# Two V stores of chunk 1 moved behind Wo's landing with one more buffer, and Wq's first quarter loaded in two halves of four heads

## The chip, the core and the metric

The kernel runs on one core of a Trainium2 chip. A core has five engines that run side by side: TensorE (PE, with its weight loads shown as PEld), VectorE (DVE), ScalarE (ACT), GpSimd (POOL) and SyncE (SP), which here does nothing but issue transfers. 16 DMA engines move data between the memory of the chip (DRAM), and the on-chip SBUF. Each engine takes its instructions in the order in which they were written for it and waits on semaphores of the others. The metric is the device time in microseconds (us), the median of several executions; lower is better.

## What is computed

The input x has 2048 rows of 512. A first block (A) normalizes the rows and runs a recurrent attention over 64 segments of 32 rows. A segment sees 8 memory rows and its own 32 rows; with 32 heads of 128 it forms queries, keys and values, a masked softmax and an output projection Wo. The first 8 rows of its output are the memory of the next segment, so the segments form a chain. A second block (B) is a gated MLP that mixes all rows by w_sp.

```python
for s in range(n_seg):
    h = concat([mem, xs], axis=1)            # 8 + 32 rows
    q, k, v = h @ Wq, h @ Wk, h @ Wv         # 32 heads x 128
    p = softmax(where(mask, q @ k.T * scale, -1e9))
    o = (p @ v) @ Wo
    mem = o[:, :M]                           # memory of the next segment
    outs.append(o[:, M:])
h = x + concat(outs)
h2 = h + B(layernorm(h))                     # gelu, spatial mix with w_sp, gate, w_out
```

All data is bfloat16 with float32 accumulation.

## The kernel before

**An emitter and its order.** The whole kernel is written as a list of operations (`Emitter.add`, line 53). Each names its engine and tokens for what it reads and writes; an operation waits for the last writer of each token that it reads, and for the last writer and all readers since of each token that it writes. A DMA is an operation of the engine that issues it (`sp`, line 274, for SP), is complete when it has landed, and counts as a reader of its source buffer until then. Within an engine the order is that of the calls.

**Loads at the start.** `load_xe` (line 301) brings the last 8 rows of each of the 16 segments of a chunk (a chunk is 16 segments). Wq, Wk, Wv and Wo are 4 MB each. `load_w` (line 305) loads a quarter, 8 of the 32 heads. The quarters of Wq (lines 318 to 321) are split by the rows of the contraction between the queues of SP and ACT; those of Wv and Wk (lines 896 to 899) go by SP alone, and the quarters of Wo (lines 921 to 923) by SP behind these. In DRAM the piece of one row of Wq, Wk or Wv that a quarter takes is 8 heads x 128 x 2 bytes; that of Wo is 512 x 2 bytes for each head and row.

**Work ahead of segment 0.** `start_group` (line 878) runs a group of matmuls into one of four PSUM banks and evacuates it on ACT or DVE in turn. `start_x` (line 889) calls `qkx_full` (line 443), which projects the rows of a chunk for four heads of Q (groups i = 0 to 7) or K (8 to 15); the matmuls are line 449. Its reads name the token of a quarter of the weight and, for Q, of its half on ACT's queue. `start_v` calls `vx_mm` (line 469, matmuls on line 476) and `vx_evac` (line 480).

**V of a chunk and its buffers.** `vx_evac(ck, n, ...)` copies group n of chunk ck to SBUF and stores it to DRAM (`vext_d`), from where `load_vx` (line 509) brings it back for each segment. Chunk 0 uses the eight slices of `part`; the other chunks take the two buffers of `Vs` in turn, by the counter `vcnt` (lines 484 to 486). A store of chunks 1 to 3 has 128 KB. For groups 2 to 7 of chunk 0 the rows of segments 2 to 5 are not stored at once: the calls are kept in `vrest[0]`, and line 1097 emits them in segment 0 with a wait for the landing of Wo's last quarter; `vrest[1]` holds the rest.

**Segment 0.** The loop over segments is at line 1015. In segment 0 the projections of the segment alternate with remaining groups of chunk 0. Line 1069 makes group 0 of chunk 1, (1,0), evacuated by DVE; line 1083 makes (1,1), evacuated by ACT at line 1096. Behind it SP gets the six stores of `vrest[0]`, `wT_read(0, 0)` (line 849, a transposing load of a block of w_sp) and `load_xe(3, 1)`; line 1106 adds the load of x block 2 (`load_x`, read by `ln_inplace`, statistics on line 367). Towards the end of the segment come (1,2), from the list `gx`, evacuated by DVE (line 490), and (2,0), from the list `gv`, evacuated by ACT (line 488) at line 1191. The output projection `Wo` (line 702) has its matmuls on line 708. Behind the evacuation of (2,0) ACT has, in this order, `S_mask(0)` (line 574), which fills the score bank of the next segment, and that segment's five `QK_evac` copies (line 550), which DVE transposes (line 558) for the score matmuls of `S_half` (lines 590 and 596). PE has the projections of the next segment (line 539) ahead of these scores.

**partx.** A buffer of 128 x 512 that `WoX_evac` (line 781) writes for the first time in segment 6 and `px_store` (line 772) stores.

Of the kernel before, what the change touches and what calls it, by code (L numbers as in the profile page):

```python
# [169 lines left out]
def fast_path(nc, st, keep, flags, A_x, A_mem0, A_Wq, A_Wk, A_Wv, A_Wo, A_seg_len, B_w_in, B_w_sp, B_b_sp, B_w_out, out):  # L170
# [3 lines left out]
    DH = A_Wq.shape[2]  # L174
# [21 lines left out]
    em = Emitter(n_dma_sems=40)  # L196

    def sb(name, shape, dt):
        return st.enter_context(nc.sbuf_tensor("f_" + name, shape, dt))
# [19 lines left out]
    hTe = sb("hTe", [128, NCK, DC, 128], BF)  # L219
# [12 lines left out]
    partx = sb("partx", [128, 512], BF)  # L232
# [38 lines left out]
    def PB(b):  # L271
        return ("ps", b)

    def sp(fn, **k):
        return em.add("sp", fn, dma=True, **k)

    def pe(fn, **k):
        return em.add("pe", fn, **k)

    def act(fn, **k):  # L280
        return em.add("act", fn, **k)

    def dve(fn, **k):
        return em.add("dve", fn, **k)
# [13 lines left out]
    def xbuf(j):  # L298
        return (xn[:, j, :], [("xn", j)]) if j < 2 else (part[:, j, :], [("part", j, 0), ("part", j, 1)])

    def load_xe(ck, j, queue="sp"):
        t, tok = xbuf(j)
        em.add(queue, lambda e: e.dma_start(t, xe[CK * ck:CK * ck + CK, XM:SEG, :]), dma=True, writes=tok)

    def load_w(mi, hq, queues=("sp",)):
        parts = len(queues)
        n = DC // parts
        wd, ws = ((A_Wq, w_q), (A_Wk, w_k), (A_Wv, w_v))[mi]
        wr = wd.rearrange("(dc p) h e -> p dc (h e)", p=128)
        cols = slice(hq * 8 * DH, (hq + 1) * 8 * DH)  # L310
        for k in range(parts):
            tok = ("W", mi, hq) if k == 0 else ("W", mi, hq, k)
            em.add(queues[k], lambda e, k=k: e.dma_start(ws[:, k * n:(k + 1) * n, cols], wr[:, k * n:(k + 1) * n, cols]), dma=True, writes=[tok])  # L313
            em.mark_const(tok)

    load_xe(0, 0)
    load_xe(1, 1, "act")
    for hq in range(4):
        load_w(0, hq, ("sp", "act"))
        if hq == 1:  # L320
            act(lambda e: e.preload_act_table_set("natural_log_exp_and_others"))
    load_x(0, 4)
# [120 lines left out]
    def qkx_full(ck, i, bank):  # L443
        mi, h0 = i // 8, 4 * (i % 8)
        ws = (w_q, w_k)[mi]
        for hh in range(4):
            h = h0 + hh
            for dc in range(DC):
                pe(lambda e, h=h, dc=dc, hh=hh: e.matmul(ps[:, bank, hh * 128:(hh + 1) * 128], lhsT=ws[:, dc, h * DH:(h + 1) * DH],
                                                         rhs=hTe[:, ck, dc, :], start=(dc == 0), stop=(dc == DC - 1)),  # L450
                   reads=[("hTe", ck), ("W", mi, h // 8) if mi or dc < 2 else ("W", mi, h // 8, 1)], writes=[PB(bank)])

    def qkx_full_evac(ck, i, bank, eng):
        mi, h0 = i // 8, 4 * (i % 8)
# [25 lines left out]
    def vx_evac(ck, n, bank, eng="act", queue="sp"):  # L480
        if ck == 0:
            t, tok = part[:, n, :], [("part", n, 0), ("part", n, 1)]
        else:
            j = vcnt[0] % 2
            vcnt[0] += 1
            t, tok = Vs[:, j, :], [("Vs", j)]
        if eng == "act":
            act(lambda e: e.activation(out=t, in_=ps[:, bank, :], func=ACT.Copy, scale=VSC), reads=[PB(bank)], writes=tok)
        else:
            dve(lambda e: e.tensor_scalar(out=t, in0=ps[:, bank, :], scalar1=VSC, scalar2=None, op0=ALU.mult), reads=[PB(bank)], writes=tok)  # L490
        def store(i0, i1, ks, queue="sp", after=()):
            r = slice(8 * i0, 8 * i1)
            dst = vext_d[ck, n, r, :, :].rearrange("p r e -> p (r e)")
            em.add(queue, lambda e: e.dma_start(dst, t[r, :]), dma=True, reads=tok, writes=[("vext", ck, n, k) for k in ks], after=after)

        if ck:
            store(0, CK, (0,), queue)
        else:
            store(0, 2, (0,), queue)
            if n < 2:  # L500
                store(2, CK, (1, 2))
            else:
                vrest[0].append(lambda after=(): store(2, 6, (1,), after=after))
                vrest[1].append(lambda: store(6, CK, (2,)))

    vcnt, vrest = [0], ([], [])
# [247 lines left out]
    def behind():  # L754
        return [em.by_eng["pe"][-1]]
# [19 lines left out]
    def px_load(rb):  # L775
        i0 = 4 * rb % 8
        for g in range(4):
            sp(lambda e, g=g: e.dma_start(part[32 * g:32 * g + M, i0:i0 + 4, :], px_d[rb, g].rearrange("j r d -> r j d")),
               reads=[("pxd", rb)] + [("part", i0 + j, k) for j in range(4) for k in range(2)], writes=[("pm", rb % 2, g)])
# [69 lines left out]
    def wT_read(i, k):  # L849
        r = slice(8 * k, 8 * k + 8)  # L850
        sp(lambda e: e.dma_start_transpose(out=wst[:, r, :], in_=B_w_sp[i * 64:(i + 1) * 64, 1024 * k:1024 * k + 1024]),
           writes=[("wst", k)], after=behind())
# [36 lines left out]
    def start_x(ck, i):  # L889
        start_group(qkx_full, qkx_full_evac, ck, i)  # L890

    def start_v(n, ck=0):
        start_group(vx_mm, vx_evac, ck, n)

    ln_apply(1)
    for hq in (0, 2, 1, 3):
        load_w(2, hq)
    for hq in range(4):
        load_w(1, hq)
# [21 lines left out]
    for hq in range(4):  # L921
        sp(lambda e, hq=hq: e.dma_start(w_o[:, 8 * hq:8 * hq + 8, :], wor[:, 8 * hq:8 * hq + 8, :]), writes=[("Wo", hq)])  # L922
        em.mark_const(("Wo", hq))


    class Gap:
# [23 lines left out]
    def vx_group(ck, n):  # L950
        gx.append([lambda dc=dc: vx_mm(ck, n, XB, dc) for dc in range(DC)] + [lambda: vx_evac(ck, n, XB, "dve")])

    def vx_atoms(ck, n):
        mms = [lambda ck=ck, n=n, dc=dc: vx_mm(ck, n, VXB, dc) for dc in range(DC)]
        gv.add(VXB, mms, lambda eng: vx_evac(ck, n, VXB, eng))
# [59 lines left out]
    for s in range(NSEG):  # L1015
# [3 lines left out]
            w2_load()  # L1019
        if j4 == 3 and rb > 0:  # L1020
            px_load(rb - 1)
        if s > 0:
            wT_read(s // 2, s % 2)

        def qk_piece(pi):
            QK(s, QKP[pi], range(2 if pi < 2 else 1 if pi == 2 and s else 0, DC))
# [67 lines left out]
        sm_rcp(1)  # L1094
        if s == 0:
            vx_evac(1, 1, 5, "act")
            for f in vrest[0]:
                f([em.last_w[("Wo", 3)]])
            wT_read(0, 0)
            load_xe(3, 1)  # L1100
        if s > 0:
            v_second()
        if j4 == 1:
# [210 lines left out]
    for i, rb in enumerate(order):  # L1314
# [8 lines left out]
        if i == 1:  # L1323
            pe(lambda e: e.matmul(ps[:, CB, :], lhsT=Sc[:], rhs=partx[:], start=True, stop=True),
               reads=["partx", "Sc"], writes=[PB(CB)])
# [52 lines left out]
    for tb in range(NTB):  # L1378
        for fb in range(len(ACC) if tb == 0 else 0, FB):
            bank = 5 + fb % 3 if tb == 0 else (tb * FB + fb) % 2  # L1380
# [688 lines left out]
def build_kernel(nc, A_x, A_mem0, A_Wq, A_Wk, A_Wv, A_Wo, A_seg_len, B_x, B_w_in, B_w_sp, B_b_sp, B_w_out, out):  # L2069
    args = (A_x, A_mem0, A_Wq, A_Wk, A_Wv, A_Wo, A_seg_len, B_w_in, B_w_sp, B_b_sp, B_w_out, out)  # L2070
    flags = {}
    with contextlib.ExitStack() as keep:
        with contextlib.ExitStack() as st:
            em, sems, dsems = fast_path(nc, st, keep, flags, *args)
# [83 lines left out]
```

## Time and profile before

| | us |
|---|---|
| median of 3 runs | 838.24 |
| lowest and highest | 837.37, 839.92 |
| the profiled execution | 840.62 |
| its span, first to last instruction | 838.9 |
| mean granted TensorE clock | 0.997 |

A row of the timeline has the start in us from the span's start, the time in us, the engine (with a q where only its sequencer works, as in issuing a DMA), the line of the kernel, the operation, what it writes and reads, the shape and how many in a row are merged; brackets show the idle time of the engine just before it and what ended it. A row of the chain of waits has start, time and what. A row of the windows has a stretch, the busy time and count of PE, PEld, DVE, ACT and POOL, then the granted clock, the busy share of the DMA engines and GB/s. A row of waits has the sum in us, how often, and the longest.

### The profile page before, as it was taken

To read this page: it belongs to the slowest core of one execution; us is meant where nothing else is said; L and a number is where in the kernel's file an instruction comes from. 1 tells how busy PE (TensorE), PEld (TensorE's weight loads), DVE (VectorE), ACT (ScalarE), POOL (GpSimd) and SP (SyncE) were. 2 spreads that over 40 slices of the span, in tenths; PEclk is the share of its full clock that TensorE was granted. 3 is DMA by queue.
4 is the path that set the end of the run, shared out by engine and by line. 5 is a ranking of instruction groups with operands and counts; after the bars stand their busy time and mean duration, and the time that the engine had idled before them with its cause. 6 is when DMAs were issued, how large, how long until landed. Compare 5 with 4: busy or idle time off the path is not lost.

```text
span 838.9 us, 48365 instructions
## 1 busy us (share of the span) xinstructions
PE 824.4 (98%) x21963; PEld 484.4 (58%) x21963; DVE 475.9 (57%) x1221; ACT 514.2 (61%) x1549; POOL 145.0 (17%) x412
## 2 busy tenths in 40 slices
PE   7999999999999999999999999999999999999998
PEld 7755565656566555655566656555665554444443
DVE  3546565656566555666556556565655576653344
ACT  2467777777777777777777777676666676300000
POOL 5202111121121111112211121111111123200000
PEclk9999999999999999999999999999999999999999
DMA  9975222122222222222212122333343278223101
GB/s 313 386 214 108 69 60 68 49 68 60 61 63 58 65 60 65 63 73 58 67 50 72 48 70 72 103 85 85 78 83 84 73 253 260 90 101 103 42 13 48
DMA packets 107652, 80.54 MB, mean 96 GB/s; under 512 B 49672, under 2 KB 97040, under 8 KB 107440
## 3 DMA queue, kind: packets, MB, share of 16 engines
q1 hardware_dynamic: 105712, 74.82, 30.8%
q8 instruction: 174, 2.85, 1.5%
q10 hardware_dynamic: 1504, 2.36, 0.9%
q14 instruction: 38, 0.31, 0.1%
q0 software_dynamic: 224, 0.20, 0.1%
HBM read 43.72 MB, written 23.13 MB: 80 GB/s over the span
## 4 chain that ended last, share of the span: by engine, by line
PE 92%; SPq 5%; DMA 1%; issue 0%; ACT 0%; DVE 0%; POOL 0%; POOLq 0%
PE f_ps L539 27%; PE f_ps L708 14%; PE f_ps L645 13%; PE f_ps L1266 12%; PE f_ps L426 4%; PE f_ps L764 4%; SPq L313 3%; PE f_ps L1360 3%; PE f_ps L1259 3%; PE f_ps L670 3%; PE f_ps L476 2%; PE f_ps L830 2%; PE f_ps L590 1%; DMA f_arena<-in_A_Wo_dram 1%; SPq L922 1%; PE f_ps L1226 1%
## 5 line engine op out<-in xcount | busy, mean ns | idle before, releaser
L539 PE MATMUL f_ps<-f_arena,f_hT 128*32 128x512 bf16 (+1 forms) x5120 | 238.5, 337 | 0.4
L539 PEld LDWEIGHTS f_ps<-f_arena,f_hT 128*32 128x32 bf16 x5120 | 124.4, 96 | 89.0 <-ACT f_hT L738 20.0
L550 ACT ACTIVATE f_Tst<-f_ps 128x512 bf16<-128x512 f32 (+2 forms) x320 | 143.4, 510 | 36.1 <-PE f_ps L539 28.5
L645 PE MATMUL f_ps<-f_arena,f_hT 128*32 128x512 bf16 x2048 | 139.8, 379 | 0.0
L708 PE MATMUL f_ps<-f_arena,f_cT 128*32 128x256 bf16 x4096 | 130.1, 273 | 2.2 <-DMA f_arena<-in_A_Wo_dram 1.3
L635 POOL TENSOR_TENSOR f_E_sb<-f_R_sb,f_E_sb 128x64 bf16<-128x64 f32 x128 | 47.5, 371 | 411.0 <-ACT f_R_sb L627 411.0
L708 PEld LDWEIGHTS f_ps<-f_arena,f_cT 128*32 128x32 bf16 x4096 | 97.0, 96 | 27.5 <-ACT f_cT L694 17.3
L558 DVE STREAM_TRANSPOSE f_QT<-f_Tst 128x256 uint32<-128x256 uint32 x128 | 57.1, 446 | 93.2 <-ACT f_Tst L550 93.2
L657 DVE TENSOR_SCALAR f_V_sb<-f_ps 128x512 bf16<-128x512 f32 (+1 forms) x128 | 71.4, 558 | 52.4 <-PE f_ps L645 52.4
L1266 PE MATMUL f_ps<-f_arena 128*128 128x512 bf16 x448 | 100.5, 379 | 0.0
L1266 PEld LDWEIGHTS f_ps<-f_arena 128*128 128x128 bf16 x448 | 43.7, 98 | 52.9 <-issue 0.3
L694 ACT ACTIVATE f_cT<-f_ps 128x160 bf16<-128x160 f32 (+1 forms) x192 | 55.6, 329 | 26.0 <-PE f_ps L676 25.4
L696 DVE TENSOR_SCALAR f_cT<-f_ps 128x256 bf16<-128x256 f32 x128 | 48.4, 420 | 36.7 <-PE f_ps L676 36.7
L604 ACT ACTIVATE f_E_sb<-f_ps 128x224 bf16<-128x224 f32 x128 | 46.3, 362 | 36.6 <-PE f_ps L616 35.4
L727 ACT ACTIVATE f_part<-f_ps 128x256 bf16<-128x256 f32 x128 | 49.3, 385 | 20.6 <-PE f_ps L708 16.1
L558 DVE STREAM_TRANSPOSE f_KT<-f_Tst 128x256 uint32<-128x256 uint32 (+2 forms) x192 | 58.4, 330 | 4.5 <-ACT f_Tst L550 1.8
L645 PEld LDWEIGHTS f_ps<-f_arena,f_hT 128*32 128x32 bf16 x2048 | 47.1, 95 | 19.8 <-issue 0.4
L738 ACT ACTIVATE f_hT<-f_ps 128x16 bf16<-128x16 f32 x126 | 23.3, 185 | 45.8 <-PE f_ps L735 45.8
L1272 DVE TENSOR_TENSOR f_arena<-f_ps,f_arena 128x512 f32<-128x512 f32 x28 | 19.3, 690 | 52.5 <-PE f_ps L1266 50.5
L627 ACT ACTIVATE f_R_sb<-f_R_sb 128x160 f32<-128x160 f32 x128 | 43.3, 338 | 4.0
L576 DVE CAST f_ps<-f_mask 128x224 f32<-128x224 bf16 x80 | 29.9, 373 | 26.9 <-ACT f_hT L406 24.5
L426 PE MATMUL f_ps<-f_arena,f_hTe 128*32 128x512 bf16 x640 | 41.9, 379 | 0.0
(127 smaller groups left out, 1157.8 us busy)
## 6 DMA issues: line engine op xcount, KB each, us to landing
wT_d<-f_wst SPq DMA_DIRECT2D x64, 128.0 KB
f_arena<-wT_d SPq DMA_DIRECT2D x32, 256.0 KB
f_arena<-in_A_Wv_dram SPq DMA_DIRECT2D x4, 1024.0 KB
f_arena<-in_A_Wk_dram SPq DMA_DIRECT2D x4, 1024.0 KB
f_arena<-in_A_Wo_dram SPq DMA_DIRECT2D x4, 1024.0 KB
f_Vx<-vext_d SPq DMA_DIRECT2D x62, 64.0 KB
vext_d<-f_Vs SPq DMA_DIRECT2D x24, 128.0 KB
zp_d<-f_Vs SPq DMA_DIRECT2D x20, 112.0 KB
```

The source lines that it names most:

```text
L426: pe(lambda e, c=c, rhs=rhs: e.matmul(ps[32 * c:32 * c + 32, bank, :], lhsT=hTe[:, ck, dc, 32 * sg:32 * sg + 32], rhs=rhs, start=(dc == 0) ...
L539: pe(lambda e, dc=dc, c=c, rhs=rhs: e.matmul(ps[32 * c:32 * c + 32, bank, 0:32 * nh], lhsT=hT[:, sl, dc, :], rhs=rhs, start=(dc == 0), sto ...
L550: act(lambda e: e.activation(out=st_.rearrange("p (hp i r) -> p hp i r", i=32, r=2), in_=ps[:, bank, 0:64 * np_].rearrange("p (hp r i) -> ...
L558: dve(lambda e: e.transpose(out=dst, in_=src), reads=tok, writes=[(nm, b, k) for k in halves(b, p0, np_)])
L635: pool(lambda e: e.tensor_tensor(out=ev, in0=rv, in1=ev, op=ALU.mult), reads=[("R", b), ("Ex", b)], writes=[("Ex", b)])
L645: pe(lambda e, dc=dc, c=c, c0=c0: e.matmul(ps[32 * c:32 * c + 32, bank, 0:w], lhsT=hT[:, sl, dc, :], rhs=w_v[:, dc, c0:c0 + w], start=(dc ...
L657: dve(lambda e: e.tensor_scalar(out=dst, in0=src, scalar1=VSC, scalar2=None, op0=ALU.mult), reads=[PB(bank)], writes=tok)
L694: act(lambda e: e.activation(out=dst, in_=src, func=ACT.Copy, scale=UNSC), reads=[PB(bank)], writes=tok)
L696: dve(lambda e: e.tensor_scalar(out=dst, in0=src, scalar1=UNSC, scalar2=None, op0=ALU.mult), reads=[PB(bank)], writes=tok)
L708: pe(lambda e, h=h, g=g, i=i, b=b, c=c: e.matmul(ps[32 * g:32 * g + 32, bank, 0:d1 - d0], lhsT=cTh[:, i, 8:40], rhs=w_o[:, h, d0:d1], star ...
L727: act(lambda e: e.activation(out=part[:, s % 8, d0:d1], in_=ps[:, bank, 0:d1 - d0], func=ACT.Copy), reads=[PB(bank)], writes=[("part", s % ...
L1266: pe(lambda e: e.matmul(ps[:, bank, 0:TB], lhsT=z2[:, sc, fb * 128:(fb + 1) * 128], rhs=wTb[tb % 2][:, :, sc, :], start=first, stop=last), ...
```

## The change

`load_w` can load half of a quarter's heads (`u` is 0 or 1), and Wq's first quarter is loaded so: four DMAs, each of half the bytes, in place of two. Group i = 0 of Q reads the token of the first half alone.

Group (1,0) is put in `partx` in place of a buffer of `Vs`, so that the counter of `Vs` starts with (1,1). The six stores of `vrest[0]` are emitted right behind the loads of Wo, ahead of the loop over segments, still with their wait for Wo's last quarter; SP takes its DMAs in order, so the stores of (1,0) and (1,1) now follow them. `wT_read(0, 0)` and `load_xe(3, 1)` are emitted at the top of segment 0 and stay behind the six stores.

```diff
--- before.py
+++ after.py
@@ -302,21 +302,22 @@
         t, tok = xbuf(j)
         em.add(queue, lambda e: e.dma_start(t, xe[CK * ck:CK * ck + CK, XM:SEG, :]), dma=True, writes=tok)
 
-    def load_w(mi, hq, queues=("sp",)):
+    def load_w(mi, hq, queues=("sp",), u=None):
         parts = len(queues)
         n = DC // parts
         wd, ws = ((A_Wq, w_q), (A_Wk, w_k), (A_Wv, w_v))[mi]
         wr = wd.rearrange("(dc p) h e -> p dc (h e)", p=128)
-        cols = slice(hq * 8 * DH, (hq + 1) * 8 * DH)
+        cols = slice(hq * 8 * DH, (hq + 1) * 8 * DH) if u is None else slice(4 * u * DH, 4 * (u + 1) * DH)
         for k in range(parts):
-            tok = ("W", mi, hq) if k == 0 else ("W", mi, hq, k)
+            tok = ("Wh", k) if u == 0 else ("W", mi, hq) if k == 0 else ("W", mi, hq, k)
             em.add(queues[k], lambda e, k=k: e.dma_start(ws[:, k * n:(k + 1) * n, cols], wr[:, k * n:(k + 1) * n, cols]), dma=True, writes=[tok])
             em.mark_const(tok)
 
     load_xe(0, 0)
     load_xe(1, 1, "act")
     for hq in range(4):
-        load_w(0, hq, ("sp", "act"))
+        for u in (None,) if hq else (0, 1):
+            load_w(0, hq, ("sp", "act"), u)
         if hq == 1:
             act(lambda e: e.preload_act_table_set("natural_log_exp_and_others"))
     load_x(0, 4)
@@ -448,7 +449,7 @@
             for dc in range(DC):
                 pe(lambda e, h=h, dc=dc, hh=hh: e.matmul(ps[:, bank, hh * 128:(hh + 1) * 128], lhsT=ws[:, dc, h * DH:(h + 1) * DH],
                                                          rhs=hTe[:, ck, dc, :], start=(dc == 0), stop=(dc == DC - 1)),
-                   reads=[("hTe", ck), ("W", mi, h // 8) if mi or dc < 2 else ("W", mi, h // 8, 1)], writes=[PB(bank)])
+                   reads=[("hTe", ck), ("Wh", dc // 2) if i == 0 else ("W", mi, h // 8) if mi or dc < 2 else ("W", mi, h // 8, 1)], writes=[PB(bank)])
 
     def qkx_full_evac(ck, i, bank, eng):
         mi, h0 = i // 8, 4 * (i % 8)
@@ -480,6 +481,8 @@
     def vx_evac(ck, n, bank, eng="act", queue="sp"):
         if ck == 0:
             t, tok = part[:, n, :], [("part", n, 0), ("part", n, 1)]
+        elif (ck, n) == (1, 0):
+            t, tok = partx[:], ["partx"]
         else:
             j = vcnt[0] % 2
             vcnt[0] += 1
@@ -921,6 +924,8 @@
     for hq in range(4):
         sp(lambda e, hq=hq: e.dma_start(w_o[:, 8 * hq:8 * hq + 8, :], wor[:, 8 * hq:8 * hq + 8, :]), writes=[("Wo", hq)])
         em.mark_const(("Wo", hq))
+    for f in vrest[0]:
+        f([em.last_w[("Wo", 3)]])
 
 
     class Gap:
@@ -1019,8 +1024,9 @@
             w2_load()
         if j4 == 3 and rb > 0:
             px_load(rb - 1)
-        if s > 0:
-            wT_read(s // 2, s % 2)
+        wT_read(s // 2, s % 2)
+        if s == 0:
+            load_xe(3, 1)
 
         def qk_piece(pi):
             QK(s, QKP[pi], range(2 if pi < 2 else 1 if pi == 2 and s else 0, DC))
@@ -1094,10 +1100,6 @@
         sm_rcp(1)
         if s == 0:
             vx_evac(1, 1, 5, "act")
-            for f in vrest[0]:
-                f([em.last_w[("Wo", 3)]])
-            wT_read(0, 0)
-            load_xe(3, 1)
         if s > 0:
             v_second()
         if j4 == 1:
```

## The prediction

> **What bounds the kernel now.** I read the page first, then the chain of waits, then the rows of each engine in the first 70 us, where every edit lies.
>
> ```profile
> span 838.9 us, 48365 instructions
> PE 824.4 (98%) x21963; PEld 484.4 (58%) x21963; DVE 475.9 (57%) x1221; ACT 514.2 (61%) x1549; POOL 145.0 (17%) x412
> ```
>
> PE is busy for 98% of the span, so a gain is either idle PE time removed or nothing. The chain of waits has PE to itself from 55.01 us on; before that it runs back through SP's loads:
>
> ```profile
> 42.84 12.13 DMA f_arena<-in_A_Wo_dram
> 55.01 1.38 PE f_ps L708 x44
> ...
> 57.40 3.05 PE f_ps L539 x72
> ```
>
> Wo's last quarter, whose issue starts at 42.84, lands at 42.84 + 12.13 = 54.97, and that landing starts everything behind it. The timeline shows the PE waits that the change touches (the second row is of the weight loads):
>
> ```profile
> 10.65 1.57 PE L449 MATMUL f_ps<-f_hTe,f_arena 128*128 128x128 bf16 x16 [3.31 <-DMA f_arena<-in_A_Wq_dram]
> 31.21 3.17 PEld L476 LDWEIGHTS f_ps<-f_arena,f_hTe 128*32 128x32 bf16 x64 [0.33 <-issue]
> 53.17 0.55 PE L708 MATMUL f_ps<-f_arena,f_cT 128*32 128x256 bf16 x12
> 55.01 1.38 PE L708 MATMUL f_ps<-f_arena,f_cT 128*32 128x256 bf16 x44 [1.29 <-DMA f_arena<-in_A_Wo_dram]
> 57.25 3.20 PE L539 MATMUL f_ps<-f_arena,f_hT 128*32 128x512 bf16 x72
> 60.28 0.27 PE L590 MATMUL f_ps<-f_QT,f_KT 128*32 128x40 bf16 x16
> ```
>
> PE waits 3.31 us for Wq's first quarter and 1.29 us for Wo's last. The 60.28 row is the first score matmul of segment 1.
>
> **Wq's first quarter in halves.** Each half asks for half the bytes, so group 0 can start earlier than 10.65, by 3.31 us at the very most (the whole wait) and by 0 at least. Either end is worth 0 on the end of the kernel: PE only reaches the 55.01 wait sooner, and Wo's landing ends that. What covers the lead is this wait of 1.29 us, which grows by it; without that cover the lead would count. The start is chased by loads throughout:
>
> ```profile
> 15.00:41.00 26.00, 26.00 (x468) 20.73 (x466) 14.96 (x34) 12.68 (x27) 8.61 (x25) 1.00 1.06 383
> 41.00:51.00 10.00, 10.00 (x239) 7.15 (x240) 4.43 (x11) 5.80 (x15) 1.23 (x3) 1.00 1.08 332
> 51.00:55.00 4.00, 2.44 (x80) 1.03 (x71) 1.22 (x5) 1.99 (x8) 1.18 (x4) 1.00 0.52 174
> ```
>
> The last two columns are the DMA engines' busy share and GB/s: they are full until 51 us. The halves do not change the bytes, but a row piece of Wq shrinks from 8 heads (2 KB) to 4 (1 KB). Wv and Wk move in 2 KB pieces (first row, 383 / 1.06 = 361 GB/s per full share), Wo in 1 KB pieces (second row, 332 / 1.08 = 307). By these 1.05 MB would take 3.42 instead of 2.90 us, +0.5 us on all behind it; the second stretch also holds other transfers, so I take **+0.2 us** on Wo's landing.
>
> The two added DMA issues (one on SP, one on ACT) cost 3.35 / 4 = 0.8 and 2.19 / 2 = 1.1 us of queue time:
>
> ```profile
> 1.56 3.35 SPq L313 DMA_DIRECT2D f_arena<-in_A_Wq_dram  x4
> 2.71 2.19 ACTq L313 DMA_DIRECT2D f_arena<-in_A_Wq_dram  x2
> 6.83 0.60 ACT L411 ACTIVATE f_hTe<-f_ps 128x512 bf16<-128x512 bf16 x1 [2.87 <-PE f_ps L387]
> 19.78 0.68 DVE L367 BATCH_NORM_STATS2 f_st<-f_part 128x6 f32<-128x512 bf16 x1
> ```
>
> ACT idles 2.87 us before its first work, which hides its issue and the table load behind it; the x loads pushed on SP are first read at 19.78. If that cover were gone, it would be up to 1.1 us of a start that Wo's landing hides anyway. Nothing for both.
>
> **The V stores behind Wo.** Today SP issues two 128 KB stores of chunk 1's V, (1,0) and (1,1), before it blocks on Wo's landing; the six held-back stores of chunk 0 follow, then a transposing load of w_sp, the x rows of chunk 3, x block 2:
>
> ```profile
> 50.15 2.17 SPq L494 DMA_DIRECT2D vext_d<-f_Vs  x2
> 54.99 3.31 SPq L494 DMA_DIRECT2D vext_d<-f_part  x6
> 58.34 1.33 SPq L851 DMA_TRANSPOSE f_wst<-in_B_w_sp_dram  x1
> 59.71 0.57 SPq L303 DMA_DIRECT2D f_xn<-in_A_x_dram  x1
> 60.33 0.58 SPq L295 DMA_DIRECT2D f_xn<-in_A_x_dram  x1
> 61.72 1.80 SPq L494 DMA_DIRECT2D vext_d<-f_Vs  x2
> 63.57 0.92 SPq L494 DMA_DIRECT2D vext_d<-f_part  x2
> ```
>
> After the change the blocking six stand ahead of everything in segment 0, so (1,0) and (1,1) come last: at 60.33, where x block 2 stands now, and 0.92 / 2 = 0.46 us later, at **60.8**. That is 9 us later than now for (1,1).
>
> Does Wo land earlier without them? At most by their bytes: 0.262 MB / 332 GB/s = 0.8 us. But (1,0) was queued after Wo and landed after it:
>
> ```profile
> 55.36 0.69 DVE L490 TENSOR_SCALAR f_Vs<-f_ps 128x512 bf16<-128x512 f32 x1 [1.59 <-DMA vext_d<-f_Vs]
> 57.57 0.59 ACT L488 ACTIVATE f_Vs<-f_ps 128x512 bf16<-128x512 f32 x1
> 58.05 0.37 ACT L574 ACTIVATE f_ps<-f_mask 128x224 f32<-128x224 bf16 x1
> 58.55 2.32 ACT L550 ACTIVATE f_Tst<-f_ps 128x512 bf16<-128x512 f32 x5
> 59.18 0.45 DVE L558 STREAM_TRANSPOSE f_QT<-f_Tst 128x256 uint32<-128x256 uint32 x1 [3.13 <-ACT f_Tst L550]
> ```
>
> DVE's wait for that store ended at 55.36, behind 54.97. So I take 0 of the 0.8. The Trainium skill, "DMA: Bandwidth & Descriptors", section "Queues, rings and completion order", speaks against this part of the change: on each DMA engine one queue's descriptors are consumed in ring order, so a store queued behind Wo would take nothing from it; by that rule the sum keeps the 0, by bytes alone it would be 0.8 us less.
>
> **The buffer that the hold keeps.** The Vs pair now rotates one step earlier: (1,1) takes Vs 0, (1,2) takes Vs 1, and the next, (2,0), takes Vs 0 again. Today (1,2) takes Vs 0 (DVE's 1.59 us wait above) and (2,0) takes Vs 1, free by then: the 57.57 row shows no wait. DVE's wait goes and is worth 0, as DVE idles 3.13 us before its next work at 59.18. In its place ACT's copy of (2,0) must wait until (1,1)'s store, issued at 60.8, has landed. How long a 128 KB store takes is bounded by SP's own wait on the stores of partx:
>
> ```profile
> SPq L778 <- DMA px_d<-f_partx: 23.1, 12, 2.8
> 115.79 0.32 SPq L773 DMA_DIRECT2D px_d<-f_partx  x1
> 118.88 1.31 SPq L778 DMA_DIRECT2D f_part<-px_d  x4
> ```
>
> The mean is 23.1 / 12 + 0.32 = 2.2 us, the slowest 2.8 + 0.3 = 3.1; in a full queue (1,0) took 55.36 − 50.15 = 5.2. The queue after 55 is nearly empty but holds the transposing load and x rows, so I take 2.5: landing at **63.3** (63.0 to 66.0).
>
> ACT works in order. Behind the copy stand the mask of score bank 3 (L574) and the five copies of Q and K (L550); behind these DVE's transposes and PE's scores, and PE, in order too, has only the 72 projection matmuls (57.25 + 3.20 = 60.45) before them. From ACT's copy to the scores it takes 60.28 − 57.57 = 2.71 us now; I take 2.65, as the projections will be done. Scores at 63.3 + 2.65 = 65.95 against 60.28: **+5.7 us**, of PE idle with nothing to hide it (5.4 to 8.4 by the bounds). Zero is excluded unless the store lands before 57.57.
>
> **The clock after such a gap.** These rows are busy time by engine with PEclk third from the end:
>
> ```profile
> 7.60:11.00 3.40, 0.35 (x7) 0.38 (x8) 0.00 (x0) 0.00 (x0) 2.38 (x13) 1.00 1.04 375
> 11.00:14.40 3.40, 3.40 (x36) 3.40 (x34) 0.89 (x2) 0.60 (x2) 2.37 (x11) 0.50 1.05 399
> 14.40:17.80 3.40, 3.40 (x63) 3.40 (x62) 1.49 (x4) 1.84 (x4) 2.65 (x11) 1.00 1.06 360
> 52.00:55.40 3.40, 2.10 (x80) 1.28 (x84) 0.93 (x4) 1.08 (x5) 0.64 (x2) 1.00 0.35 123
> ```
>
> After 3.4 us in which PE worked 0.35, the granted clock stood at 0.50 for 3.4 us, and PE did 36 matmuls instead of 63: 3.4 x (1 − 36/63) = 1.5 us lost. A stretch with 2.10 us of work lost nothing. A gap from 60.45 to 65.95 holds such an empty stretch, but part of the slow time may still lie in the gap: 0 to 1.5, I take **+1.2 us**. The Trainium skill, "TensorE: Matmul & The Clock Gate", Part 1, has windows of 3413 ns that run freely and halve the rate after an idle one; by it the loss depends on the window's phase, between 0.7 and 1.7 us, and the sum would stay within 0.5 us.
>
> Other moved steps: w_sp's transposing load and the x rows of chunk 3 keep their place behind the six stores, worth 0; x block 2 is issued about 0.95 us later, and DVE reads it in segment 1, itself 5.7 us later, worth 0 (uncovered 0.95). Partx is written next in segment 6; its store then is the 115.79 row.
>
> **Sum.** 5.7 + 1.2 + 0.2 + 0 = +7.1 us. The profiled execution took 840.62 us, its span 838.9; the median is 838.24, and I add the difference to that: **845.3 us**.
>
> **The rivals.**
> 1. *The stall without the clock loss.* For it: the slow stretch may fall inside the gap or not come. Against: the 0.50 row. 838.24 + 5.9 = 844.1.
> 2. *A longer stall.* The store lands in a full queue as (1,0) did: 66.0, scores at 68.65, +8.4; with 0.2 and 1.5 that is 848.3. For it: load of w_sp ahead of it. Against: only 174 GB/s even before 55.
> 3. *Not slower: Wo lands early.* The place is Wo's last quarter: from 51 to 55 the share is 0.52, so some DMA engines finish late, and if the two stores hold these up, Wo may come far sooner. PE then gains its 1.29 us: 836.95. As SP's line takes 63.3 − 54.97 = 8.3 us from Wo's landing to the store's, this decides only if Wo lands by 57.57 − 8.3 = 49.3, 5.7 us earlier; 0.8 us is what the bytes are worth.
> 4. *The change does not do what it says:* the hold keeps no buffer in the way, because ACT's copy is ordered otherwise, and Wo lands as before: 838.4. Against: the 1.59 us that DVE waits for just such a store now.
>
> **How the numbers follow.** Forecast 0.60, rival 1 0.20, rival 2 0.10, rival 3 0.04, rival 4 0.06. The range of 842.0 to 848.3 takes in the first three with their bounds (Wo 0.8 us earlier, a store 0.5 us quicker). A measurement can tell about 0.3%, 2.5 us, from no change. Slower holds the first three, 0.90; rivals 3 and 4 lie within 0.3%, except that the halves' lead might add to rival 3: same 0.07, faster 0.03.
>
> **What would show it.** ACT's L488 at about 63 with an idle of some 5.5 us put down to DMA vext_d<-f_Vs; SP's row for f_Vs x2 at about 60.3, behind the f_part x6; PE idle before L590 of segment 1; PEclk 0.50 for a stretch after 64; PE's first L449 before 10.65 and a longer wait for Wo. Wrong would be an ACT copy at 57.6 without a wait, or Wo landing before 54.

## The result and the profile after

| | before | after |
|---|---|---|
| median of 6 runs each, us | 837.75 | 846.29 |
| lowest and highest, us | 837.31, 839.92 | 844.42, 848.59 |
| the profiled execution, us | 840.62 | 844.42 |
| its span, us | 838.9 | 842.7 |

The changed kernel is slower: ratio 1.010, 95% interval 1.0082 to 1.0119. The profiled execution of after, 844.42, is the lowest of its six, and that of before, 840.62, lies above all six of its times, so the two spans differ by 3.8 us where the medians differ by 8.5. The time is therefore read stage by stage.

The chain of waits of after, from 30 to 76 us, still has Wo's landing in it; a V store (`DMA vext_d<-f_Vs`) now stands there too, as the shares by line show:

```profile
by line: DMA f_arena<-in_A_Wo_dram 26.5%; SPq L925 19.6%; PE f_ps L542 11.8%; PE f_ps L477 10.1%; PE f_ps L648 7.5%; PE f_ps L711 7.5%; DMA vext_d<-f_Vs 4.4%; ACT f_Tst L553 2.2%; SPq L497 1.8%; ACT f_part L491 1.3%; ACT f_Vs L491 1.3%; SPq
```

PE's timeline of after (line numbers have moved by 1 to 3: L450 is the Q and K projection of a chunk, L711 is Wo, L542 the projections of a segment, L593 the scores):

```profile
8.29 1.86 PE L450 MATMUL f_ps<-f_hTe,f_arena 128*128 128x128 bf16 x16 [0.73 <-DMA f_arena<-in_A_Wq_dram]
29.72 3.64 PE L477 MATMUL f_ps<-f_arena,f_hTe 128*32 128x512 bf16 x64 [0.46 <-issue]
53.90 1.39 PE L711 MATMUL f_ps<-f_arena,f_cT 128*32 128x256 bf16 x44 [1.39 <-DMA f_arena<-in_A_Wo_dram]
56.14 3.20 PE L542 MATMUL f_ps<-f_arena,f_hT 128*32 128x512 bf16 x72
64.21 0.32 PE L593 MATMUL f_ps<-f_QT,f_KT 128*32 128x40 bf16 x16 [4.87 <-DVE f_KT L561]
73.66 3.20 PE L542 MATMUL f_ps<-f_arena,f_hT 128*32 128x512 bf16 x72
```

The first group starts at 8.29 in place of 10.65, and PE still waits 1.39 us for Wo. New is the gap of 4.87 us ahead of segment 1's scores. DVE's transpose ended it, but the reason stands one engine further back, in ACT's timeline:

```profile
56.38 0.18 ACT L741 ACTIVATE f_hT<-f_ps 128x16 bf16<-128x16 f32 x1 [0.37 <-PE f_ps L738]
61.83 0.60 ACT L491 ACTIVATE f_Vs<-f_ps 128x512 bf16<-128x512 f32 x1 [5.27 <-DMA vext_d<-f_Vs]
62.32 0.36 ACT L577 ACTIVATE f_ps<-f_mask 128x224 f32<-128x224 bf16 x1
62.60 2.31 ACT L553 ACTIVATE f_Tst<-f_ps 128x512 bf16<-128x512 f32 x5
```

ACT stands 5.27 us before the copy of (2,0), until the store of (1,1) out of the same Vs buffer has landed. SP's timeline shows why that store is late:

```profile
53.88 3.24 SPq L497 DMA_DIRECT2D vext_d<-f_part  x6
57.16 1.32 SPq L854 DMA_TRANSPOSE f_wst<-in_B_w_sp_dram  x1
58.53 0.57 SPq L303 DMA_DIRECT2D f_xn<-in_A_x_dram  x1
59.15 0.58 SPq L497 DMA_DIRECT2D vext_d<-f_partx  x1
59.78 0.43 SPq L497 DMA_DIRECT2D vext_d<-f_Vs  x1
60.25 0.46 SPq L295 DMA_DIRECT2D f_xn<-in_A_x_dram  x1
```

The six stores start when Wo has landed, and (1,1) is issued at 59.78, 5.9 us behind that. It lands at 61.83, after 2.05 us. The windows of after (last three columns: granted clock, DMA share, GB/s; the first number after the length is PE's busy time) show the second cost:

```profile
4.90:8.30 3.40, 1.43 (x20) 1.06 (x18) 1.79 (x6) 0.60 (x1) 2.51 (x8) 1.00 0.95 296
8.30:11.70 3.40, 3.40 (x33) 3.40 (x34) 0.89 (x2) 0.60 (x1) 2.35 (x12) 0.50 1.05 400
59.50:62.90 3.40, 0.00 (x0) 0.00 (x0) 0.00 (x0) 1.07 (x3) 0.00 (x0) 1.00 0.70 231
62.90:66.30 3.40, 2.09 (x56) 1.02 (x60) 1.96 (x6) 2.17 (x6) 0.00 (x0) 0.50 0.44 125
66.30:69.70 3.40, 3.40 (x72) 1.52 (x60) 1.70 (x4) 1.91 (x6) 0.92 (x3) 0.50 0.09 27
69.70:73.10 3.40, 3.40 (x136) 2.21 (x128) 2.27 (x6) 1.64 (x7) 0.45 (x2) 1.00 0.26 79
```

A stretch without any PE work is followed by two at half the clock: 72 matmuls where the next stretch does 136. From segment 1's scores to the 72 projections of segment 2 it takes 73.66 − 64.21 = 9.45 us. In the profile of before that end point is this row of PE's timeline, 7.14 us behind the scores at 60.28:

```profile
67.42 3.20 PE L539 MATMUL f_ps<-f_arena,f_hT 128*32 128x512 bf16 x72
```

So the half clock cost 2.31 us in this profile. By segment 2 the changed kernel is 73.66 − 67.42 = 6.24 us behind. What follows is the same code in both, 838.9 − 67.42 = 771.5 us before and 842.7 − 73.66 = 769.0 after: the rest of the program took 2.5 us less in the profile of after, and no edit lies there.

### The profile page after: what moved, and what is told of

It reads as the page before. It is cut to its first block, busy times and chain, and to the rows that moved or that the text cites. A ratio compares the mean times of both kernels' runs of the same rounds, so it can differ in the third digit from the quotient of the medians.

```text
span 842.7 us, 48369 instructions
## 1 busy us (share of the span) xinstructions
PE 826.1 (98%) x21963; PEld 487.2 (58%) x21963; DVE 475.2 (56%) x1221; ACT 512.8 (61%) x1549; POOL 144.5 (17%) x412
## 3 DMA queue, kind: packets, MB, share of 16 engines
q10 hardware_dynamic: 1776, 2.36, 0.9%
## 4 chain that ended last, share of the span: by engine, by line
PE 94%; DMA 3%; SPq 1%; ACT 1%; issue 0%; DVE 0%; ACTq 0%
PE f_ps L542 26%; PE f_ps L711 14%; PE f_ps L648 13%; PE f_ps L1268 11%; PE f_ps L427 4%; PE f_ps L767 4%; PE f_ps L477 3%; PE f_ps L1362 3%; PE f_ps L1261 3%; PE f_ps L673 3%; PE f_ps L450 2%; PE f_ps L833 2%; PE f_ps L593 1%; DMA f_arena<-in_A_Wo_dram 1%; PE f_ps L1228 1%; SPq L925 1%
## 5 line engine op out<-in xcount | busy, mean ns | idle before, releaser
L542 PE MATMUL f_ps<-f_arena,f_hT 128*32 128x512 bf16 (+1 forms) x5120 | 238.3, 337 | 0.2
L542 PEld LDWEIGHTS f_ps<-f_arena,f_hT 128*32 128x32 bf16 x5120 | 126.9, 96 | 86.9 <-ACT f_hT L741 19.5
L648 PE MATMUL f_ps<-f_arena,f_hT 128*32 128x512 bf16 x2048 | 141.6, 383 | 0.2 <-issue 0.2
L711 PE MATMUL f_ps<-f_arena,f_cT 128*32 128x256 bf16 x4096 | 130.0, 273 | 1.8 <-DMA f_arena<-in_A_Wo_dram 1.4
L711 PEld LDWEIGHTS f_ps<-f_arena,f_cT 128*32 128x32 bf16 x4096 | 96.4, 96 | 27.3 <-ACT f_cT L697 18.3
L648 PEld LDWEIGHTS f_ps<-f_arena,f_hT 128*32 128x32 bf16 x2048 | 47.9, 96 | 20.6 <-issue 1.3
L593 PEld LDWEIGHTS f_ps<-f_QT,f_KT 128*32 128x32 bf16 x2048 | 28.3, 95 | 23.5 <-DVE f_KT L561 22.9
```

The costliest lines, as they stand in the source:

```text
L542: pe(lambda e, dc=dc, c=c, rhs=rhs: e.matmul(ps[32 * c:32 * c + 32, bank, 0:32 * nh], lhsT=hT[:, sl, dc, :], rhs=rhs, start=(dc == 0), sto ...
L648: pe(lambda e, dc=dc, c=c, c0=c0: e.matmul(ps[32 * c:32 * c + 32, bank, 0:w], lhsT=hT[:, sl, dc, :], rhs=w_v[:, dc, c0:c0 + w], start=(dc ...
L711: pe(lambda e, h=h, g=g, i=i, b=b, c=c: e.matmul(ps[32 * g:32 * g + 32, bank, 0:d1 - d0], lhsT=cTh[:, i, 8:40], rhs=w_o[:, h, d0:d1], star ...
```

## The experiments

Two theories: *theory 1*, ACT's copy of (2,0) waits for the held store of (1,1), PE idles behind it and its clock falls; *theory 2*, the loss is in the smaller pieces of Wq's halves or in SP's order as such. Edits are against the changed kernel unless said otherwise, ratios against the kernel before on the same chip.

| run | ratio, 95% interval | median, us | before, us |
|---|---|---|---|
| the kernel before again | 0.9995, 0.9979 to 1.0010 | 839.76 | 839.46 |
| the halves alone | 1.0004, 0.9989 to 1.0019 | 840.53 | 839.46 |
| the hold undone | 0.9993, 0.9977 to 1.0008 | 838.80 | 839.46 |
| own buffer for (1,1) | 1.0023, 1.0008 to 1.0038 | 841.69 | 839.46 |
| own buffers for (1,1), (1,2) | 1.0028, 1.0006 to 1.0050 | 838.59 | 836.71 |
| two loads later | 1.0050, 1.0033 to 1.0067 | 839.98 | 836.71 |
| the hold alone | 1.0106, 1.0083 to 1.0128 | 843.79 | 836.71 |
| gap filled, 18 matmuls | 1.0123, 1.0106 to 1.0140 | 845.43 | 836.71 |
| the changed kernel again | 1.0064, 1.0039 to 1.0089 | 847.24 | 842.43 |
| gap filled, 12 matmuls | 1.0054, 1.0035 to 1.0072 | 846.65 | 842.43 |

**The kernel before again.**

> The kernel before, unchanged, to see how far two executions differ and where Wo's last quarter lands in another one. Both theories: ratio 1.000 within 0.003, PE's wait for Wo between 0.5 and 2 us, Wo landing within 1.5 us of 54.97, no PE idle over 1 us after it.

PE's timeline has one row for all 56 first Wo matmuls, without a wait for Wo:

```profile
53.42 1.99 PE L708 MATMUL f_ps<-f_arena,f_cT 128*32 128x256 bf16 x56
56.26 3.20 PE L539 MATMUL f_ps<-f_arena,f_hT 128*32 128x512 bf16 x72
59.29 0.27 PE L590 MATMUL f_ps<-f_QT,f_KT 128*32 128x40 bf16 x16
```

So the wait for Wo that was expected did not come: in this execution Wo had landed in time. SP's six stores, which wait for the same landing, start at 54.00 in place of 54.99. When Wo lands differs by that much between executions of one kernel; a gain or loss of less cannot be read off a pair of profiles.

**The halves alone** (the kernel before, with the change of `load_w`, its loop and the reads of `qkx_full`, and nothing else).

```diff
...
     for hq in range(4):
-        load_w(0, hq, ("sp", "act"))
+        for u in (None,) if hq else (0, 1):
+            load_w(0, hq, ("sp", "act"), u)
```

> The kernel before with Wq's first quarter in halves and nothing else. Theory 1: PE's first projection starts 1 to 3 us earlier, PE waits that much longer for the last Wv quarter and for Wo, and the time is within 0.3% of before (ratio 0.997 to 1.003). Theory 2: 1 to 8 us slower than before.

PE's timeline:

```profile
8.19 1.05 PE L450 MATMUL f_ps<-f_hTe,f_arena 128*128 128x128 bf16 x16 [0.71 <-DMA f_arena<-in_A_Wq_dram]
9.97 1.96 PE L450 MATMUL f_ps<-f_hTe,f_arena 128*128 128x128 bf16 x32 [0.50 <-DMA f_arena<-in_A_Wq_dram]
12.72 10.89 PE L450 MATMUL f_ps<-f_hTe,f_arena 128*128 128x128 bf16 x192 [0.79 <-DMA f_arena<-in_A_Wq_dram]
30.93 3.64 PE L477 MATMUL f_ps<-f_arena,f_hTe 128*32 128x512 bf16 x64 [1.78 <-issue]
54.65 1.39 PE L709 MATMUL f_ps<-f_arena,f_cT 128*32 128x256 bf16 x44 [0.83 <-DMA f_arena<-in_A_Wo_dram]
```

The first group starts 2 us sooner (8.19 against 10.23 in the kernel before again; how much of this the halves gave is not certain, since in the run of the hold alone, with the quarter loaded whole, the group started at 8.49), and PE hands the lead back in later waits: 0.50 and 0.79 us for Wq, 1.78 at 30.93, 0.83 for Wo. No change of time, as theory 1 has it.

**The hold undone.**

```diff
-    for f in vrest[0]:
-        f([em.last_w[("Wo", 3)]])
...
-        wT_read(s // 2, s % 2)
-        if s == 0:
-            load_xe(3, 1)
+        if s > 0:
+            wT_read(s // 2, s % 2)
...
             vx_evac(1, 1, 5, "act")
+            for f in vrest[0]:
+                f([em.last_w[("Wo", 3)]])
+            wT_read(0, 0)
+            load_xe(3, 1)
```

> The changed kernel with the hold undone: the six stores, w_sp's transposing load and the x rows are emitted behind (1,1)'s evacuation again; the halves and the new rotation of Vs with partx stay. Theory 1: (1,1) is stored at about 50 and has landed before 57, so ACT's copy of (2,0) waits under 0.5 us and the time is within 0.3% of before. A rival that blames the rotation alone: ACT still waits for Vs 0 and the time stays over 842.

SP's and ACT's timelines:

```profile
51.83 0.34 SPq L497 DMA_DIRECT2D vext_d<-f_Vs  x1
54.73 3.29 SPq L497 DMA_DIRECT2D vext_d<-f_part  x6
```

```profile
57.31 0.59 ACT L491 ACTIVATE f_Vs<-f_ps 128x512 bf16<-128x512 f32 x1
```

With (1,1) stored at 51.83, ACT copies (2,0) at 57.31 without a wait, and the time is that of before. The halves and the new rotation without the hold cost nothing; the hold makes the loss.

**The hold alone** (Wq's first quarter loaded whole again, with `load_w` and the reads of `qkx_full` as before).

```diff
...
-        for u in (None,) if hq else (0, 1):
-            load_w(0, hq, ("sp", "act"), u)
+        load_w(0, hq, ("sp", "act"))
```

> The changed kernel with Wq's first quarter loaded whole again: hold and rotation alone. Theory 1 (the hold and the rotation make all of the loss): 845 to 848, ratio 1.007 to 1.012, and ACT's wait for Vs between 4.5 and 6 us. Theory 2 (the halves have a share): at least 2 us faster than the changed kernel, ratio under 1.006.

ACT's timeline:

```profile
60.69 0.60 ACT L490 ACTIVATE f_Vs<-f_ps 128x512 bf16<-128x512 f32 x1 [5.61 <-DMA vext_d<-f_Vs]
```

The same wait, and a ratio within the first interval of the changed kernel (by the two medians alone it would be 1.0085). The median, 843.79, is below the 845 to 848 that were expected, but that of before is lower on this chip too; by the ratio the expectation holds, and theory 2 falls for the halves.

**Own buffer for (1,1).**

```diff
             t, tok = partx[:], ["partx"]
+        elif (ck, n) == (1, 1):
+            t, tok = hbuf[:, 1, :], [("h", 1)]
```

> The changed kernel, but (1,1) is put in the second half of hbuf, unused until segment 5, so that (2,0) finds a free Vs; the hold and the halves stay. Theory 1 (ACT's copy of (2,0) waits for the held store of (1,1), PE idles behind it and the clock falls): ACT's wait and PE's 4.87 us gap are gone, PEclk stays 1.00 after 60 us, and the time is 837 to 839, as before. Theory 2 (the loss is in the order of SP's queue or in the 1 KB pieces of Wq): still 844 to 848.

ACT's, DVE's and PE's timelines:

```profile
56.67 0.59 ACT L493 ACTIVATE f_Vs<-f_ps 128x512 bf16<-128x512 f32 x1
68.28 0.60 ACT L493 ACTIVATE f_Vs<-f_ps 128x512 bf16<-128x512 f32 x1 [1.33 <-DMA vext_d<-f_Vs]
```

```profile
67.96 0.69 DVE L495 TENSOR_SCALAR f_Vs<-f_ps 128x512 bf16<-128x512 f32 x1 [3.76 <-DMA vext_d<-f_Vs]
```

```profile
59.38 0.27 PE L595 MATMUL f_ps<-f_QT,f_KT 128*32 128x40 bf16 x16
71.62 0.28 PE L595 MATMUL f_ps<-f_QT,f_KT 128*32 128x40 bf16 x16 [1.82 <-DVE f_KT L563]
```

The gap ahead of segment 1 is gone, and with it most of the loss; theory 1 holds for it. But the time stays 0.2% over before and misses the 837 to 839 us expected: one segment later ACT waits 1.33 us and DVE 3.76 us for the next stores of Vs in SP's late line. DVE, which does its transposes behind this, ends PE's idle time of 1.82 us ahead of segment 2's scores. The clock falls behind it (granted 0.50 from 73.2 to 76.6 us): segment 2 takes 80.55 − 71.62 = 8.93 us from its scores to the next 72 projections.

**Own buffers for (1,1) and (1,2)** (the edit above, and one more).

```diff
+        elif (ck, n) == (1, 2):
+            t, tok = xo[:, 1, :], [("xo", 1)]
```

> The changed kernel with (1,1) in the second half of hbuf and (1,2) in the second half of xo, both unused until later segments; hold and halves stay. In the run with one buffer of its own a second, smaller wait had appeared in segment 1: DVE's copy of (1,3) for (1,2)'s store, 3.8 us, and ACT's of (2,1), with 1.82 us of PE idle and 0.5 of the clock for one stretch. Theory 1 (all of the loss is waits for Vs buffers that the late line of SP keeps): no PE idle over 1 us after Wo's wait, ratio 0.997 to 1.002. If SP's late line costs in another way too: ratio still 1.002 or more, with an idle at another place.

PE's timeline has segments 1 and 2 in the time of before, 7.13 and 7.00 us from the scores to the next projections, and no gap (segment 1 shown):

```profile
60.26 0.27 PE L597 MATMUL f_ps<-f_QT,f_KT 128*32 128x40 bf16 x16
67.39 3.20 PE L546 MATMUL f_ps<-f_arena,f_hT 128*32 128x512 bf16 x72
```

Yet the ratio, 1.0028, misses the 0.997 to 1.002 expected, if by little. The profiled execution took 837.46 us, one of the lower ones of this kernel, and shows nothing to blame. What costs the held kernel the last 0.1 to 0.5% without a visible wait stays open.

**Two loads later.**

```diff
-        wT_read(s // 2, s % 2)
-        if s == 0:
-            load_xe(3, 1)
+        if s > 0:
+            wT_read(s // 2, s % 2)
...
             vx_evac(1, 1, 5, "act")
+            wT_read(0, 0)
+            load_xe(3, 1)
```

> The changed kernel with w_sp's transposing load and the x rows of chunk 3 emitted behind the two V stores again, so that SP reaches (1,1) about 1.32 + 0.57 + 0.1 = 2 us sooner. Theory 1 (the price is the landing of (1,1), us for us): ACT's wait falls from 5.3 to about 3.0 us (the transposing load no longer lies ahead of the store on the way), PE's gap from 4.9 to about 2.6, the clock may still fall, and the time is 842 to 845. If the wait were not the price: still 845 to 847.

ACT's and PE's timelines:

```profile
59.83 0.60 ACT L491 ACTIVATE f_Vs<-f_ps 128x512 bf16<-128x512 f32 x1 [2.81 <-DMA vext_d<-f_Vs]
```

```profile
62.21 0.28 PE L593 MATMUL f_ps<-f_QT,f_KT 128*32 128x40 bf16 x16 [2.42 <-DVE f_KT L561]
69.23 3.20 PE L542 MATMUL f_ps<-f_arena,f_hT 128*32 128x512 bf16 x72
```

With two transfers fewer ahead of (1,1), ACT waits 2.81 us in place of 5.27 and PE 2.42 in place of 4.87. The shorter gap left the clock at full: 69.23 − 62.21 = 7.02 us to the next projections. Beside the hold alone on the same chip the loss halves (1.0050 against 1.0106); the time, 839.98, is still below the 842 to 845 us expected. The price follows the landing of (1,1), as theory 1 has it.

**The gap filled.**

```diff
+        if s == 1:
+            for _ in range(18):
+                pe(lambda e: e.matmul(ps[:, WXB, :], lhsT=onesrc[:, 0:128], rhs=w_q[:, 0, 0:512], start=True, stop=True),
+                   reads=["onesrc"], writes=[PB(WXB)])
```

> The changed kernel with 18 matmuls of 128x512 into an unused PSUM bank ahead of segment 1's first scores: about 18 x 0.22 = 3.9 us of PE work in its gap of 4.87 us, which adds to what is computed and changes no output. If the clock's fall is a cost of its own behind the stall: PEclk stays 1.00 through 60 to 72 us, segment 1 takes about 2.2 us less, and the time is 843 to 845. If the gap is the whole cost: no change, 845.5 to 847.5. If the fill runs longer than the gap: slower than 847.

PE's timeline:

```profile
54.82 2.54 PE L711 MATMUL f_ps<-f_arena,f_cT 128*32 128x256 bf16 x44 [2.07 <-DMA f_arena<-in_A_Wo_dram]
61.71 4.06 PE L1066 MATMUL f_ps<-f_arena,f_onesrc 128*128 128x512 bf16 x18
65.70 0.28 PE L593 MATMUL f_ps<-f_QT,f_KT 128*32 128x40 bf16 x16
72.53 3.20 PE L542 MATMUL f_ps<-f_arena,f_hT 128*32 128x512 bf16 x72
```

In the trace segment 1 runs at full clock, 6.83 us from the scores to the next projections against 9.45. But here the clock had fallen earlier, behind the wait of 2.07 us for Wo (44 matmuls took 2.54 us in place of 1.39), and the fill ran right up to the scores. The profiled execution, 840.91 us, is also the lowest of its five by 4 us. The ratio, 1.0123, is no better: the expected 843 to 845 us was missed. So a shorter fill was run beside the changed kernel.

**The changed kernel again, and a fill of 12** (`range(12)`).

> The changed kernel, unchanged, to see a second execution of it beside the next one. Both theories: ratio 1.008 to 1.012, ACT's wait for Vs 4.5 to 6 us, PE's gap 4.5 to 5.5 us, a clock of 0.50 for one or two stretches of 3.4 us after it, and 19.9 to 22.5 us from segment 1's scores to segment 3's (20.4 before).

> The fill again with 12 matmuls in place of 18, 12 x 0.22 = 2.6 us, so that it ends well ahead of the scores' operands; in the run with 18 it ended at 65.70, at about the time when they were ready, and the clock had fallen ahead of it, after a wait of 2.07 us for Wo. If the clock's fall in segment 1 costs time of its own: 1 to 2.5 us less than the changed kernel in the same batch, ratio to it 0.997 to 0.999. If the time is only that of the stall: the same as the changed kernel within 1 us.

PE's timelines, the changed kernel first:

```profile
65.03 0.33 PE L593 MATMUL f_ps<-f_QT,f_KT 128*32 128x40 bf16 x16 [5.33 <-DVE f_KT L561]
74.23 3.20 PE L542 MATMUL f_ps<-f_arena,f_hT 128*32 128x512 bf16 x72
```

```profile
65.32 0.28 PE L593 MATMUL f_ps<-f_QT,f_KT 128*32 128x40 bf16 x16 [2.58 <-DVE f_KT L561]
72.58 3.20 PE L542 MATMUL f_ps<-f_arena,f_hT 128*32 128x512 bf16 x72
```

The stretch takes 9.20 us without and 7.26 with the fill, which never lets PE idle a whole stretch. That is 1.9 us in the trace. The medians, 847.24 and 846.65, differ by 0.6 us, less than the bounds of either ratio, where 1 to 2.5 us were expected if the clock costs time of its own: its cost is shown in the traces and not in the timed runs. The changed kernel's ratio on this chip, 1.0064, misses the 1.008 to 1.012 expected and is below its first, 1.0082 to 1.0119; the interval reaches only to 1.0089; the loss in medians was 8.5 us in the first comparison and 4.8 in this one.

No version was faster than the kernel before beyond its interval.

## Why the prediction was right

Predicted were 845.3 us and a range of 842.0 to 848.3; measured were 846.29. By its own steps:

- **What bounds the kernel**: right. PE's chain starts at Wo's landing, before and after.
- **Halves of Wq worth 0**: right, shown by the halves alone (1.0004). The first group started 2.36 us sooner in the profile of after, within the bound of 3.31 (how much of it the halves gave stays open), and the lead went back into later waits, among them those at 29.72 and for Wo.
- **Wo 0.2 us later by 1 KB pieces, 0 us earlier by the stores' absence**: neither can be seen. Wo landed 1.1 us earlier in the profile of after (53.88 against 54.97), but the kernel before again had it as early without the change (54.00).
- **(1,1) stored at 60.8 and landed at 63.3**: the order on SP was right. From Wo's landing to ACT's copy it took 61.83 − 53.88 = 7.95 us against 8.3; the store took 2.05 us against the 2.5 assumed.
- **The stall, +5.7 us**: right in mechanism. From PE's restart at Wo to the scores it took 64.21 − 53.90 = 10.31 us against 60.28 − 55.01 = 5.27 before: +5.04. Besides the quicker store, ACT's copy to scores took 2.38 us in place of the 2.65 assumed (2.71 before): ACT's copies of Q and K began 0.77 us behind it in place of 0.98, and the scores came 0.50 us behind the start of DVE's transpose of K in place of 0.61.
- **The clock, +1.2 us**: right in mechanism by the profiles (the timed runs with a fill do not show it), the size was off: 2.31 us, 9.45 against 7.14. I had taken one slow stretch, partly hidden in the gap; there were two, since a stretch in which PE worked 2.09 of 3.40 us did not bring the clock back. The bound of 1.5 us was too low for the same reason. The Trainium skill, "TensorE: Matmul & The Clock Gate", Part 1, says that the full rate returns after one busy window, of about 3.4 us sustained; the trace agrees, with the 62.90 row busy for 61%, which did not restore the clock, and the 66.30 row busy throughout, which did.
- **DVE's wait worth 0, x block 2 worth 0**: nothing in the profile of after waits for either.
- **The sum**: 5.0 + 2.3 − 1.1 = 6.2 us by segment 2, against 7.1. Three misses partly cancel here: the stall 0.7 below, the clock 1.1 above, Wo 1.3 earlier. The median moved by 8.5 us in the first comparison and by 4.8 in the second, so that 846.29 came within 1 us of 845.3 is in part luck. What the first comparison lost beyond 6.2 us no profile shows.
- **Rivals**: the stall without the clock loss happened only where the gap was shortened or filled (two loads later, fill of 12). A longer stall did not come: the store landed at 61.83 and not at 66.0. Wo landing early enough, by 49.3, did not come near. The rival that the hold keeps no buffer in the way fell with the 61.83 row.

## What to carry to other kernels

Before a store is moved later in a queue, list who writes its source buffer next, and on which engine: the store holds that buffer until it has landed, and an in-order engine that waits for it holds everything behind. Moving a transfer out of the way of a load that a chain waits for gains nothing unless the load ends sooner, and here the loads were already ahead of the stores in the queue. A gap on TensorE that empties a stretch of about 3.4 us must be priced with the slow stretches behind it, and two of them, not one, when the restart is itself patchy, as here. The length of a gap alone does not tell whether the clock falls: in these profiles it fell behind 1.82 us (own buffer for (1,1)) and 2.07 us (18 matmuls), and it did not fall behind 2.42 us (two loads later).

## What was not expected

- After the gap the granted clock stood at 0.50 for two stretches of 3.4 us in both profiles of the changed kernel, with PE busy for 2.09 of 3.40 us in the first of them (1.59 in the changed kernel again).
- At the start a stretch with 1.43 us of PE work of 3.40 was followed by a slow one (the 4.90 row); so the clock falls on less than an idle stretch. Behind a wait of 2.07 us for Wo it fell too.
- In the profiles the same code behind segment 2 took between 839.2 − 72.53 = 766.7 us (fill of 18) and 846.1 − 72.58 = 773.5 us (fill of 12), 0.9% apart (own buffer for (1,1), which waits once more there, left out). This goes with the chip: it was 766.7 to 769.0 us where the kernel before had a median of 836.71, 769.8 to 772.1 where it had 839.46, and 771.6 and 773.5 where it had 842.43. So only runs beside the kernel before on the same chip can be compared.
